# Grouped 1x1 convolution on one core: a loop of GpSimd memsets out, a narrow ring piece carried by four DMA engines in

## The chip, the core and the metric

The kernel runs on one core of a Trainium2 chip. The metric is device microseconds of that core for one execution. A time given for the kernel is the median of several executions; the profile and its trace come from one of them.

## The reference

An image of 512 x 512 pixels with 192 channels in bf16 goes through a 1x1 convolution in four groups of 48 channels. With k = 1 there is no padding, and the loop over window positions has one turn:

```python
xg = x.reshape(B, H, W, 4, 48)
out = einsum('bhwgc,gcd->bhwgd', xg, w[0, 0])      # w: 1 x 1 x 4 x 48 x 48
return out.reshape(B, H, W, 192)
```

So each of the 262,144 pixels is a row of 192 numbers (384 bytes) that is multiplied by a block-diagonal 192 x 192 matrix. The input is 100.66 MB and so is the output; every byte is read once and written once.

## The kernel before

**Layout.** Pixels are put on 128 rows (partitions) of SBUF. One *column* of a ring is one pixel on each of the 128 rows, 192 bf16 values wide. All pixels make 2048 columns. There are two rings of 256 columns, `x_sb` for input and `o_sb` for output. A *piece* is a run of columns that one transfer moves; row p of a piece of `size` columns is a contiguous run of `size` pixels in DRAM, so a piece of 64 columns moves 24,576 bytes for each row and 3,072 KB in all. `plan_pieces` cuts the 2048 columns into a head of 4, 4, 8, 16, 32 columns, then 30 pieces of 64 (`BIG`), then a tail of 32, 16, 8, 4, 4. Loads and stores use the same cut: 40 loads, 40 stores.

**Groups.** The compute engines work in groups of 4 columns, 512 groups in all, so a piece of 64 columns is 16 groups. For group g:

- TensorE transposes six 128 x 128 blocks of `x_sb` into `xT_ps` (line 203), three groups ahead of the products (`LOOK = 3`).
- VectorE copies them to `xT_sb` (line 260).
- TensorE multiplies with the block-diagonal weights `wt` into `o_ps`, six matmuls (line 226).
- ScalarE copies the result to `o_sb` (line 288, 128 x 768). In every fourth group VectorE takes half of it (line 266), and ScalarE the other half (line 285).

**Order and waits.** SyncE's queue issues all loads in order (line 175). A load waits until the groups that held its place in the ring, 64 groups before, have been transposed (`wq.wait(t_done, p.g1 - body)`). TensorE waits for a load's semaphore before the first transposes of its piece; a transfer adds 16 to its semaphore in increments of 1, one for each DMA engine that has finished. ScalarE's queue issues the stores (line 275), each two groups after the last group of its piece. Before writing group g to `o_sb`, ScalarE and VectorE wait until the store of the piece that held group g - 64 has landed (`wait_out_free`). TensorE's program has a loop of 7 turns over 64 groups, with unrolled groups ahead and behind; the other engines are unrolled. 

**GpSimd.** It builds `ident` and `esel`, two constant matrices, at the start. After that it runs the loop that the change removes: 63 turns of 64 memsets of one bf16 element of `scratch` (line 164), paced by four semaphores `pa_sem` that GpSimd alone sets and waits for. No other engine reads `scratch` or these semaphores.

**DMA.** The two queues (q1 for loads from SyncE, q10 for stores from ScalarE) run on the same 16 DMA engines. In a transfer of 128 rows each DMA engine carries 8 rows.

In the text a piece is called by its first column c: the piece c = 1600 holds groups 400 to 415.

Of the kernel before, what the change touches and what calls it, by code (L numbers as in the profile page):

```python
# [6 lines left out]
BF16 = mybir.dt.bfloat16  # L7
# [4 lines left out]
C = GROUPS * CG  # L12
# [12 lines left out]
BIG = 64  # L25
RCOLS = 256
HEAD = (4, 4, 8, 16, 32)
TAIL = (32, 16, 8, 4, 4)
# [2 lines left out]
LOOK = 3  # L31
ST_DELAY = 2
RING = 8


class Waiter:

    def __init__(self, eng):
        self.eng = eng
        self.seen = {}  # L40
# [7 lines left out]

class Piece:

    def __init__(self, col, size, key):
        self.col, self.size, self.key = col, size, key
        self.g0, self.g1 = col // 4, (col + size) // 4


def plan_pieces(cols, head, tail):
    sizes = list(head) if cols >= sum(head) + sum(tail) else []
    last = list(tail) if sizes else []
    mid = cols - sum(sizes) - sum(last)
    pieces, c = [], 0  # L60
    for s in sizes + [BIG] * (mid // BIG) + ([mid % BIG] if mid % BIG else []) + last:
        whole = s == BIG and c % BIG == 0
        pieces.append(Piece(c, s, ("big", c // BIG % (RCOLS // BIG)) if whole else ("own", len(pieces))))
        c += s
    return pieces


def bass_standalone__grouped__vision_kernel(nc, x, w, out):
    B, H, W_, Cx = x.shape
    assert Cx == C and tuple(w.shape) == (1, 1, GROUPS, CG, CG)  # L70
    npix = B * H * W_

    cols = npix // 128
    assert npix % 512 == 0, "the pixel count must be a multiple of 512"
    NG = cols // 4
    loads = plan_pieces(cols, HEAD, TAIL)
    stores = plan_pieces(cols, HEAD, TAIL)
    load_of = {p.g0: p for p in loads}
    store_at = {g: p for p in stores for g in range(p.g0, p.g1)}
    store_end = {p.g1 - 1: p for p in stores}  # L80
# [1 line left out]
    xf = x.rearrange("b h w c -> (b h w) c")  # L82
    of = out.rearrange("b h w c -> (b h w) c")
# [17 lines left out]
        if 0 <= h < NG and shared(h):  # L101
            dve_prog.append(("ev2", h))

    def rows_view(ap, p):
        return ap[128 * p.col:128 * (p.col + p.size), :].rearrange("(p i) c -> p (i c)", p=128)

    def ring_view(t, p):
        at = p.col % RCOLS
        assert at + p.size <= RCOLS
        return t[:, at * C:(at + p.size) * C]  # L110

    with ExitStack() as es:
        block = es.enter_context(nc.Block())
        x_sb = es.enter_context(nc.sbuf_tensor("x_sb", [128, RCOLS * C], BF16))
        o_sb = es.enter_context(nc.sbuf_tensor("o_sb", [128, RCOLS * C], BF16))
# [2 lines left out]
        esel = es.enter_context(nc.sbuf_tensor("esel", [CG, ECOLS], BF16))  # L118
        w_sb = es.enter_context(nc.sbuf_tensor("w_sb", [CG, GROUPS, CG], BF16))
        wt = es.enter_context(nc.sbuf_tensor("wt", [128, WCOLS], BF16))  # L120
        scratch = es.enter_context(nc.sbuf_tensor("scratch", [1, 64], BF16))
        xT_ps = es.enter_context(nc.psum_tensor("xT_ps", [128, NXP, 1024], BF16))
        o_ps = es.enter_context(nc.psum_tensor("o_ps", [128, NOB, 512], F32))

        def sem(name):
            return es.enter_context(nc.semaphore(name))

        ld_sem = {k: sem(f"ld_{k[0]}{k[1]}") for k in dict.fromkeys(p.key for p in loads)}
        st_sem = {k: sem(f"st_{k[0]}{k[1]}") for k in dict.fromkeys(p.key for p in stores)}
        st_val, seen = {}, {}  # L130
        for p in stores:
            seen[p.key] = seen.get(p.key, 0) + 16
            st_val[p] = seen[p.key]
        w_sem, id_sem, e_sem, wb_sem, wc_sem = (sem(s) for s in ("w_sem", "id_sem", "e_sem", "wb_sem", "wc_sem"))
        p0_sem, p1_sem = sem("p0_sem"), sem("p1_sem")
        pa_sem = [sem(f"pa_{i}") for i in range(4)]
        t_done, mm_done = sem("t_done"), sem("mm_done")
        e1_sem = [sem(f"e1_{i}") for i in range(RING)]
        fa_sem = [sem(f"fa_{i}") for i in range(RING)]
# [7 lines left out]
        @block.gpsimd  # L147
        def _(gp):
            gp.memset(esel[:], 1.0).then_inc(p0_sem, 1)  # L149
            gp.memset(ident[:], 1.0).then_inc(p1_sem, 1)  # L150
            gp.wait_ge(p0_sem, 1)
            gp.affine_select(out=esel[:], in_=esel[:], pattern=[[-1, ECOLS]],  # L152
                             compare_op=AluOpType.is_equal, fill=0.0, base=ESHIFT,
                             channel_multiplier=1).then_inc(e_sem, 1)
            gp.wait_ge(p1_sem, 1)
            gp.affine_select(out=ident[:], in_=ident[:], pattern=[[-1, 128]],  # L156
                             compare_op=AluOpType.is_equal, fill=0.0, base=0,
                             channel_multiplier=1).then_inc(id_sem, 1)
            gp.memset(scratch[:, 63:64], 0.0).then_inc(pa_sem[0], 1)  # L159
            with gp.Fori(0, 63, 1):  # L160
                for j in range(4):
                    gp.wait_ge(pa_sem[j], 1)
                    for i in range(16):
                        ins = gp.memset(scratch[:, j * 16 + i:j * 16 + i + 1], 0.0)  # L164
                        if i == 1:
                            ins.then_inc(pa_sem[j], -1)
                    ins.then_inc(pa_sem[(j + 1) % 4], 1)

        @block.sync
        def _(sp):  # L170
            wq = Waiter(sp)
            sp.dma_start(w_sb[:], wv).then_inc(w_sem, 16)  # L172
            for p in loads:
                wq.wait(t_done, p.g1 - body)
                sp.dma_start(ring_view(x_sb, p), rows_view(xf, p)).then_inc(ld_sem[p.key], 16)  # L175

        @block.tensor
        def _(pe):

            def build_weights():  # L180
                pe.wait_ge(e_sem, 1)
                pe.wait_ge(w_sem, 16)
                last = None
                for (tc, r, g, c0_) in WBLOCKS:
                    s0 = ESHIFT - r
                    col = WOFF[tc] + c0_
                    last = pe.matmul(o_ps[:, NOB - 1, col:col + CG], lhsT=esel[:, s0:s0 + 128],  # L187
                                     rhs=w_sb[:, g, :], start=True, stop=True, skip_group_check=True)
                last.then_inc(wb_sem, 1)

            def transposes(g):
                if g == 0:
                    pe.wait_ge(id_sem, 1)
                p = load_of.get(g)
                if p:
                    pe.wait_ge(ld_sem[p.key], 16)
                ins = []
                for ul in range(2):
                    u = g % body * 2 + ul
                    for tc in range(3):  # L200
                        col = u * UC + tc * 128
                        j = ul * 3 + tc
                        ins.append(pe.transpose(xT_ps[:, g % NXP, j * 128:(j + 1) * 128],  # L203
                                                x_sb[:, col:col + 128], ident[:]))
                if p:
                    ins[1].then_inc(ld_sem[p.key], -16)
                ins[-1].then_inc(t_done, 1)

            def matmuls(g):
                xs = xT_sb[g % NXP]  # L210
                waited = [e1_sem[g % RING]]
                if g == 0:
                    pe.wait_ge(wc_sem, 1)
                if g >= 2:
                    waited.append(fa_sem[(g - 2) % RING])
                    if shared(g - 2):
                        waited.append(d2_sem[(g - 2) // 4 % 2])
                for s in waited:
                    pe.wait_ge(s, 1)
                ins = []  # L220
                for ul in range(2):
                    v = 2 * g + ul
                    for tc in range(3):
                        j = ul * 3 + tc
                        c0_, c1_ = COLR[tc]
                        ins.append(pe.matmul(o_ps[:, v % NOB, c0_:c1_], lhsT=xs[:, j * 128:(j + 1) * 128],  # L226
                                             rhs=wt[:, WOFF[tc]:WOFF[tc] + (c1_ - c0_)],
                                             start=(tc == 0), stop=(tc == 2), skip_group_check=True))
                for i, s in enumerate(waited):
                    ins[1 + i].then_inc(s, -1)  # L230
                ins[-1].then_inc(mm_done, 1)

            def step(g):
                if g + LOOK < NG:
                    transposes(g + LOOK)
                matmuls(g)

            build_weights()
            for g in range(min(LOOK, NG)):
                transposes(g)  # L240
            for g in range(loop_g0 if reps else 0):
                step(g)
            if reps:
                with pe.Fori(0, reps, 1):
                    for g in range(loop_g0, loop_g0 + body):
                        step(g)
            for g in range(loop_g1 if reps else 0, NG):
                step(g)
# [21 lines left out]
        def _(act):  # L270
# [1 line left out]
            pending = []  # L272

            def store(p):
                act.dma_start(rows_view(of, p), ring_view(o_sb, p)).then_inc(st_sem[p.key], 16)  # L275

            for g in range(NG):
                wait_out_free(wq, g)
# [5 lines left out]
                if shared(g):  # L284
                    ins = act.copy(o_sb[:, u * UC:(u + 1) * UC], o_ps[:, v % NOB, 0:UC])  # L285
# [40 lines left out]
```

## Time and profile before

| | |
|---|---|
| median of 3 executions | 497.32 us (495.99 to 498.0) |
| the profiled execution's own time | 498.0 us |
| span of its profile | 496.3 us |
| granted TensorE clock | 0.95 |
| busy: TensorE matmul / weight load | 424.2 us (85%) / 408.8 us (82%) |
| busy: ScalarE / VectorE | 356.8 us (72%) / 336.9 us (68%) |
| busy: GpSimd | 148.4 us (30%), of it 147.1 us in 4032 memsets |
| DMA | 201.64 MB, 406 GB/s over the span |

The span is the profiler's, from the first instruction to the last event; the execution's own time is 1.7 us more. Busy shares are averages over the whole span. A step that lies beside other work costs nothing; what ends a wait, and what stands in the chain that ended last, tells what sets the time.

### The profile page before, as it was taken

To read this page: it belongs to the slowest core of one execution; us is meant where nothing else is said; L and a number is where in the kernel's file an instruction comes from. 1 tells how busy PE (TensorE), PEld (TensorE's weight loads), DVE (VectorE), ACT (ScalarE), POOL (GpSimd) and SP (SyncE) were. 2 spreads that over 40 slices of the span, in tenths; PEclk is the share of its full clock that TensorE was granted. 3 is DMA by queue.
4 is the path that set the end of the run, shared out by engine and by line. 5 is a ranking of instruction groups with operands and counts; after the bars stand their busy time and mean duration, and the time that the engine had idled before them with its cause. 6 is when DMAs were issued, how large, how long until landed. Compare 5 with 4: busy or idle time off the path is not lost.

```text
span 496.3 us, 18331 instructions
## 1 busy us (share of the span) xinstructions
PE 424.2 (85%) x6154; PEld 408.8 (82%) x6154; DVE 336.9 (68%) x640; ACT 356.8 (72%) x513; POOL 148.4 (30%) x4041
## 2 busy tenths in 40 slices
PE   5999998789887998797997797997979977999953
PEld 5989998788887998787997787987879977889852
DVE  3778877577675777576776576775767765778740
ACT  2888887577775778676787586776767865888752
POOL 8999999999999100000000000000000000000000
PEclk9999999899898999899899899898998998999986
DMA  8999999999999999999999999999999999995583
GB/s 295 432 423 425 429 427 436 426 432 434 425 431 429 432 434 428 432 431 432 430 426 429 432 430 424 432 430 430 430 426 434 430 420 436 427 381 243 223 365 144
DMA packets 11751, 201.64 MB, mean 406 GB/s; under 512 B 1488, under 2 KB 2512, under 8 KB 3536
## 3 DMA queue, kind: packets, MB, share of 16 engines
q1 hardware_dynamic: 5968, 100.68, 47.8%
q10 hardware_dynamic: 5760, 100.67, 47.7%
q8 instruction: 12, 0.20, 0.1%
q14 instruction: 11, 0.09, 0.0%
HBM read 100.68 MB, written 100.66 MB: 406 GB/s over the span
## 4 chain that ended last, share of the span: by engine, by line
DMA 83%; PE 12%; another core or an unknown queue 1%; ACT 1%; issue 1%; SPq 0%; ACTq 0%
DMA out_dram<-o_sb 81%; PE o_ps L226 7%; PE xT_ps L203 5%; DMA x_sb<-in_x_dram 1%; ACT o_sb L288 1%; SPq L175 0%; ACTq L275 0%; SPq L172 0%
## 5 line engine op out<-in xcount | busy, mean ns | idle before, releaser
L288 ACT CAST o_sb<-o_ps 128x768 bf16<-128x768 f32 x385 | 301.5, 798 | 123.7 <-PE o_ps L226 69.9
L260 DVE COPY xT_sb<-xT_ps 128x768 bf16<-128x768 bf16 x512 | 284.3, 555 | 112.8 <-PE xT_ps L203 105.8
L226 PE MATMUL o_ps<-wt,xT_sb 128*128 128x144 bf16 (+1 forms) x3072 | 308.3, 238 | 52.5 <-ACT o_sb L288 50.3
L203 PE MATMUL xT_ps<-ident,x_sb 128*128 128x128 bf16 x3072 | 266.0, 225 | 9.5 <-DMA x_sb<-in_x_dram 8.9
L226 PEld LDWEIGHTS o_ps<-wt,xT_sb 128*128 128x128 bf16 x3072 | 218.2, 100 | 65.9 <-issue 57.1
L203 PEld LDWEIGHTS xT_ps<-ident,x_sb 128*128 128x128 bf16 x3072 | 206.1, 101 | 11.2 <-DMA x_sb<-in_x_dram 9.2
L164 POOL MEMSET scratch<- 1x1 bf16 x4032 | 147.1, 91 | 14.4
L266 DVE CAST o_sb<-o_ps 128x384 bf16<-128x384 f32 x127 | 69.9, 551 | 32.9 <-DMA out_dram<-o_sb 30.6
L285 ACT CAST o_sb<-o_ps 128x384 bf16<-128x384 f32 x127 | 60.9, 480 | 8.8 <-PE o_ps L226 6.5
L256 DVE CAST wt<-o_ps 128x480 bf16<-128x480 f32 x1 | 0.7, 658 | 3.3 <-PE o_ps L187 3.3
L187 PE MATMUL o_ps<-w_sb,esel 48*128 48x48 bf16 x10 | 0.6, 210 | 2.8 <-DMA w_sb<-in_w_dram 2.8
L187 PEld LDWEIGHTS o_ps<-w_sb,esel 48*128 48x128 bf16 x10 | 0.5, 113 | 2.7 <-POOL esel L152 2.7
L288 ACT ACT_TABLE_LOAD x1 | 1.3, 1283 | 0.8 <-PEq L311 0.8
L152 POOL TENSOR_SCALAR_AFFINE_SELECT esel<-esel 48x272 bf16<-48x272 bf16 x1 | 0.4, 405 | 0.0
L149 POOL MEMSET esel<- 48x272 bf16 x1 | 0.3, 318 | 0.3 <-POOLq L311 0.3
L156 POOL TENSOR_SCALAR_AFFINE_SELECT ident<-ident 128x128 bf16<-128x128 bf16 x1 | 0.3, 285 | 0.0
L150 POOL MEMSET ident<- 128x128 bf16 x1 | 0.2, 198 | 0.0
L311 POOL MEMSET const-float32-0.0<- 128x1 f32 x1 | 0.1, 103 | 0.3 <-issue 0.3
L311 POOL MEMSET const-uint8-127<- 128x1 uint8 x1 | 0.1, 116 | 0.0
L311 POOL MEMSET const-bfloat16-1.0<- 128x1 bf16 x1 | 0.1, 113 | 0.0
L311 POOL MEMSET const-float32-1.0<- 128x1 f32 x1 | 0.1, 111 | 0.0
L159 POOL MEMSET scratch<- 1x1 bf16 x1 | 0.1, 91 | 0.0
## 6 DMA issues: line engine op xcount, KB each, us to landing
x_sb<-in_x_dram SPq DMA_DIRECT2D x30, 3072.0 KB, 28.9
out_dram<-o_sb ACTq DMA_DIRECT2D x30, 3072.0 KB, 45.5
x_sb<-in_x_dram SPq DMA_DIRECT2D x2, 1536.0 KB, 20.3
out_dram<-o_sb ACTq DMA_DIRECT2D x2, 1536.0 KB, 26.4
x_sb<-in_x_dram SPq DMA_DIRECT2D x2, 768.0 KB, 22.0
out_dram<-o_sb ACTq DMA_DIRECT2D x2, 768.0 KB, 19.8
x_sb<-in_x_dram SPq DMA_DIRECT2D x4, 192.0 KB, 27.2
x_sb<-in_x_dram SPq DMA_DIRECT2D x2, 384.0 KB, 24.6
```

Of the source, the lines that this page charges most:

```text
L149: gp.memset(esel[:], 1.0).then_inc(p0_sem, 1)
L152: gp.affine_select(out=esel[:], in_=esel[:], pattern=[[-1, ECOLS]], compare_op=AluOpType.is_equal, fill=0.0, base=ESHIFT, channel_multipli ...
L164: ins = gp.memset(scratch[:, j * 16 + i:j * 16 + i + 1], 0.0)
L187: last = pe.matmul(o_ps[:, NOB - 1, col:col + CG], lhsT=esel[:, s0:s0 + 128], rhs=w_sb[:, g, :], start=True, stop=True, skip_group_check=True)
L203: ins.append(pe.transpose(xT_ps[:, g % NXP, j * 128:(j + 1) * 128], x_sb[:, col:col + 128], ident[:]))
L226: ins.append(pe.matmul(o_ps[:, v % NOB, c0_:c1_], lhsT=xs[:, j * 128:(j + 1) * 128], rhs=wt[:, WOFF[tc]:WOFF[tc] + (c1_ - c0_)], start=(tc ...
L256: dve.tensor_copy(wt[:], o_ps[:, NOB - 1, 0:WCOLS]).then_inc(wc_sem, 1)
L260: dve.tensor_copy(xT_sb[g % NXP][:], xT_ps[:, g % NXP, 0:2 * UC]).then_inc(e1_sem[g % RING], 1)
L266: dve.tensor_copy(o_sb[:, u * UC:(u + 1) * UC], o_ps[:, v % NOB, 0:UC]).then_inc(d2_sem[g // 4 % 2], 1)
L285: ins = act.copy(o_sb[:, u * UC:(u + 1) * UC], o_ps[:, v % NOB, 0:UC])
L288: ins = act.copy(dst, o_ps[:, v % NOB:v % NOB + 2, 0:UC])
L311: nc = _bacc.Bacc("TRN2", target_bir_lowering=False, num_devices=1)
```

## The change

The memset loop, `scratch` and `pa_sem` go. In their place nothing is put on GpSimd.

The cut of the pixels changes. One piece of 64 columns is *narrow*: only rows 0 to 15 and 32 to 47 hold pixels (2048 of them, as many as 16 full columns), moved by two loads and two stores of 16 rows each, whose DRAM side has an outer dimension of 4. The other pixels fill 2032 full columns. With the narrow piece's 64 the ring runs over 2096 columns, so there are 524 groups instead of 512, and the compute engines treat the narrow piece's 16 groups like any others, on all 128 rows; of its results only the 32 rows are stored. A piece may no longer cross the ring's end, so the order is: head 4, 4, 8, 16, 32; 29 pieces of 64 (up to c = 1856); the narrow piece (c = 1920); then 48, 16, 16, 16, 8, 4, 4. That is 43 loads and 43 stores. A narrow transfer pair adds 32 to its semaphore, and TensorE waits for 32.

```diff
+FULL = ((0, 128),)
+NARROW = ((0, 16), (32, 16))
+N_NARROW = 1
...
+def plan_pieces(npix):
+    few = BIG * sum(rows for _, rows in NARROW)
+    n_few = N_NARROW if npix >= N_NARROW * few + 128 * (sum(HEAD) + sum(TAIL) + 8 * BIG) else 0
+    cols = (npix - n_few * few) // 128
...
+    sizes = [(s, FULL) for s in head + [BIG] * (mid // BIG)]
+    sizes += [(BIG, NARROW)] * n_few
+    sizes += [(s, FULL) for s in ([mid % BIG] if mid % BIG else []) + tail]
...
+    def transfers(ap, t, p):
         at = p.col % RCOLS
         assert at + p.size <= RCOLS
-        return t[:, at * C:(at + p.size) * C]
+        for (r0, rows, pix) in p.blocks:
+            px = ap[pix:pix + rows * p.size, :]
+            if p.narrow:
+                view = px.rearrange("(c a i) n -> a c (i n)", a=4, c=rows // 4)
+            else:
+                view = px.rearrange("(p i) n -> p (i n)", p=rows)
+            yield view, t[r0:r0 + rows, at * C:(at + p.size) * C]
...
-            gp.memset(scratch[:, 63:64], 0.0).then_inc(pa_sem[0], 1)
-            with gp.Fori(0, 63, 1):
-                for j in range(4):
-                    gp.wait_ge(pa_sem[j], 1)
-                    for i in range(16):
-                        ins = gp.memset(scratch[:, j * 16 + i:j * 16 + i + 1], 0.0)
-                        if i == 1:
-                            ins.then_inc(pa_sem[j], -1)
-                    ins.then_inc(pa_sem[(j + 1) % 4], 1)
...
-                sp.dma_start(ring_view(x_sb, p), rows_view(xf, p)).then_inc(ld_sem[p.key], 16)
+                for dram, ring in transfers(xf, x_sb, p):
+                    sp.dma_start(ring, dram).then_inc(ld_sem[p.key], 16)
...
-                act.dma_start(rows_view(of, p), ring_view(o_sb, p)).then_inc(st_sem[p.key], 16)
+                for dram, ring in transfers(of, o_sb, p):
+                    act.dma_start(dram, ring).then_inc(st_sem[p.key], 16)
```

More of the change, by code (lines that the diff above doesn't have):

```diff
@@ L49, with __init__ @@
 class Piece:
-    def __init__(self, col, size, key):
+    def __init__(self, col, size, key, blocks, pix):
         self.col, self.size, self.key = col, size, key
         self.g0, self.g1 = col // 4, (col + size) // 4
[L56 to L64, printed above, removed]
+        self.blocks = []
+        for (r0, rows) in blocks:
+            self.blocks.append((r0, rows, pix))
+            pix += rows * size
+        self.pix_end = pix
+        self.narrow = len(blocks) > 1
+def plan_pieces(npix):
+    few = BIG * sum(rows for _, rows in NARROW)
+    n_few = N_NARROW if npix >= N_NARROW * few + 128 * (sum(HEAD) + sum(TAIL) + 8 * BIG) else 0
+    cols = (npix - n_few * few) // 128
+    assert cols % 4 == 0
+    head, tail = (list(HEAD), list(TAIL)) if cols >= sum(HEAD) + sum(TAIL) else ([], [])
+    mid = cols - sum(head) - sum(tail)
+    sizes = [(s, FULL) for s in head + [BIG] * (mid // BIG)]
+    sizes += [(BIG, NARROW)] * n_few
+    sizes += [(s, FULL) for s in ([mid % BIG] if mid % BIG else []) + tail]
+    pieces, c, pix = [], 0, 0
+    while sizes:
+        s, blocks = sizes.pop(0)
+        room = RCOLS - c % RCOLS
+        if s > room:
+            sizes.insert(0, (s - room, blocks))
+            s = room
+        whole = s == BIG and c % BIG == 0 and blocks is FULL
+        key = ("big", c // BIG % (RCOLS // BIG)) if whole else ("own", len(pieces))
+        pieces.append(Piece(c, s, key, blocks, pix))
+        c, pix = c + s, pieces[-1].pix_end
+    assert pix == npix
     return pieces
@@ L71, in bass_standalone__grouped__vision_kernel @@
     npix = B * H * W_
-    cols = npix // 128
     assert npix % 512 == 0, "the pixel count must be a multiple of 512"
-    NG = cols // 4
-    loads = plan_pieces(cols, HEAD, TAIL)
-    stores = plan_pieces(cols, HEAD, TAIL)
+    loads = stores = plan_pieces(npix)
+    NG = loads[-1].g1
     load_of = {p.g0: p for p in loads}
@@ L102, in bass_standalone__grouped__vision_kernel @@
             dve_prog.append(("ev2", h))
-    def rows_view(ap, p):
-        return ap[128 * p.col:128 * (p.col + p.size), :].rearrange("(p i) c -> p (i c)", p=128)
-    def ring_view(t, p):
+    def transfers(ap, t, p):
         at = p.col % RCOLS
         assert at + p.size <= RCOLS
-        return t[:, at * C:(at + p.size) * C]
+        for (r0, rows, pix) in p.blocks:
[5 more added lines that the diff above has]
+            yield view, t[r0:r0 + rows, at * C:(at + p.size) * C]
     with ExitStack() as es:
@@ L120, in bass_standalone__grouped__vision_kernel @@
         wt = es.enter_context(nc.sbuf_tensor("wt", [128, WCOLS], BF16))
-        scratch = es.enter_context(nc.sbuf_tensor("scratch", [1, 64], BF16))
         xT_ps = es.enter_context(nc.psum_tensor("xT_ps", [128, NXP, 1024], BF16))
@@ L131, in bass_standalone__grouped__vision_kernel @@
         for p in stores:
-            seen[p.key] = seen.get(p.key, 0) + 16
+            seen[p.key] = seen.get(p.key, 0) + 16 * len(p.blocks)
             st_val[p] = seen[p.key]
@@ L135, in bass_standalone__grouped__vision_kernel @@
         p0_sem, p1_sem = sem("p0_sem"), sem("p1_sem")
-        pa_sem = [sem(f"pa_{i}") for i in range(4)]
         t_done, mm_done = sem("t_done"), sem("mm_done")
@@ L195, in transposes @@
                 if p:
-                    pe.wait_ge(ld_sem[p.key], 16)
+                    pe.wait_ge(ld_sem[p.key], 16 * len(p.blocks))
                 ins = []
@@ L205, in transposes @@
                 if p:
-                    ins[1].then_inc(ld_sem[p.key], -16)
+                    ins[1].then_inc(ld_sem[p.key], -16 * len(p.blocks))
                 ins[-1].then_inc(t_done, 1)
```

## The prediction

> **What bounds the kernel now.** I read the page's slices first: is the DMA full all the way?
>
> ```profile
> DMA  8999999999999999999999999999999999995583
> GB/s 295 432 423 425 429 427 436 426 432 434 425 431 429 432 434 428 432 431 432 430 426 429 432 430 424 432 430 430 430 426 434 430 420 436 427 381 243 223 365 144
> ```
>
> Up to slice 35 (434 us) the 16 DMA engines are full at about 430 GB/s. Then they are half idle, for 60 us. Bandwidth as a whole doesn't explain that end. The chain of work that ended last does (start, duration, what):
>
> ```profile
> 77.94 47.15 DMA out_dram<-o_sb
> 125.12 46.77 DMA out_dram<-o_sb
> ...
> 217.53 45.54 DMA out_dram<-o_sb
> 263.11 45.58 DMA out_dram<-o_sb
> 308.72 45.47 DMA out_dram<-o_sb
> 354.22 45.55 DMA out_dram<-o_sb
> ...
> 478.36 6.17 another core or an unknown queue
> ```
>
> From store to store, each link 45 us or more, and each spans three ring pieces, so 15.2 us for one piece (64 columns loaded and 64 stored). A 24,576-byte packet takes 912 ns at the median in the packet records; 8 for the load and 8 for the store are 14.6 us. Something runs 4% slower than the typical DMA engine. The trace's completion increments (16 for each transfer, one for each DMA engine) name it: of the last load, fourteen came by 445.4 us, the fifteenth at 447.4, the sixteenth at 484.5. Of store c = 1600, fourteen by 419.7 and the last at 443.6. In all loads and stores after 70 us **one DMA engine comes last alone**, by 7 to 10 us in loads and up to 23 in stores. It also ends the run: its last stores land at 488.3, 492.1, 493.9, 494.8, 495.3 and 495.8, while the other fifteen are done by 492.4. Those steps are its packets back to back. It works from the first load to the end without a gap, so its bytes times its pace are the time. The waits up to 440 us and after agree:
>
> ```profile
> ACT o_sb L288 <- DMA out_dram<-o_sb: 51.5, 24, 3.3
> ...
> PE xT_ps L203 <- DMA x_sb<-in_x_dram: 6.2, 1, 6.2
> ```
>
> ScalarE waits for stores once for each piece; at the end TensorE waits 6.2 us for the last load (the chain's "unknown queue" at 478.36), which stood behind the late engine's stores.
>
> Second reading: the pace differs. The late engine's increments for loads come each 15.72 us from 70.0 to 164.3 us (six steps), and each 15.19 us from 179.6 to 437.8 (seventeen). The chain says the same: 47.15, then 45.5. What ends in between?
>
> ```profile
> L164 POOL MEMSET scratch<- x4032: 91/91/94, 2.1 to 163.4; 1x1 bf16 x192
> ```
>
> ```profile
> 60.00:160.00 100.00, 85.43 (x1244) 82.38 (x1242) 68.13 (x130) 71.62 (x105) 91.06 (x2499) 0.95 1.00 430
> 160.00:400.00 240.00, 210.13 (x3054) 203.50 (x3051) 167.29 (x318) 175.78 (x254) 3.24 (x90) 0.95 1.00 430
> ```
>
> The last memset starts at 163.4 us. In these windows (PE, PEld, DVE, ACT, POOL busy with counts, clock, DMA share, GB/s) nothing but GpSimd's 2499 instructions changes; the typical packet stays at 912 ns, and the late engine's store packets go from about 1040 to 985 ns.
>
> Third reading, the tail's compute, from the timeline:
>
> ```profile
> 445.22 2.35 ACT L288 CAST o_sb<-o_ps 128x768 bf16<-128x768 f32 x3 [0.38 <-PE o_ps L226]
> 448.33 2.35 ACT L288 CAST o_sb<-o_ps 128x768 bf16<-128x768 f32 x3 [0.33 <-PE o_ps L226]
> ```
>
> Four groups in 3.11 us, 0.78 a group: unhindered, a piece takes 12.5 us, under the 15.2 of the late engine. From 443.66 us (store c = 1600 has landed) to 478.36 compute runs at this pace without a stop.
>
> [...]
>
> **The change part by part.**
>
> *Twelve DMA engines carry less.* 2032 instead of 2048 full columns, 16 fewer each way. On the late engine: 16/64 x 15.19 = **3.8 us less**, if it isn't one of the four.
>
> *Four engines carry more.* 2096 columns, 48 more: 48/64 x 14.6 = 10.9 us. They had 512 packets' worth each way, 64 x 8 x 0.912 = 467 us; with this 478, and from the first load at 4.9 us that is 483 without a gap. The late engine's end will be 488 (below), and after 440 us they were idle for about half of the time. Cost 0; it decides if they get more than 5 us of idle time that the late one has not.
>
> *The memset loop goes.* Measured on the chain: (47.15 - 45.54) + (46.77 - 45.54) = 2.8 us. Before 77.9 us the loop ran too; 3.4% of the chain's first store link (39.4 us) is 1.35 more. **4.2 us less**. Bounds: 0 if something else changed at 160 us, 5.5 if all of 2.1 to 163.4 us ran 3.4% slow. A loss could only come if the memsets sped something, and nothing slows after 163 us. GpSimd has no other work.
>
> *Twelve more groups*, 9.4 us of compute at 0.78. Ahead of the tail it lies beside DMA. In the tail it doesn't: see the sum.
>
> *Queues and waits.* SyncE issues 43 loads for 40, but waited 408.6 us for TensorE; 0. ScalarE issues 3 more stores at 0.34 us: up to 1.0 us in the tail. TensorE's wait for 32 has the products of group 477 and on behind it; the four engines have the narrow load before about 435 us and group 480 comes at about 451: 0, and up to 7 us if it were late. No later group reuses the narrow piece's output place.
>
> *The sum.* Late engine: 495.8 - 3.8 - 4.2 = 487.8 us. Compute: store c = 1536, which frees group 448, landed at 430.1, now at 425.9. Its 16 groups take 12.5 us, to 438.4. Store c = 1600 landed at 443.6, now at 437.5 to 439.4 (4.2 earlier, and up to 1.9 for the shorter load ahead of it). So group 464 starts at 438.4 to 439.4; 60 groups to the end at 0.78 are 46.8: 485.2 to 486.2. Add 1.0 for the issues and 2.1 from ScalarE's end to the landing (490.1 to 492.2 before): 488.3 to 489.3. The last load now lands in time, since no big store stands beside it: the 6.2 us wait goes, and **compute is late next, by about a microsecond**. The span ends 0.5 after the last landing: 489.3, which is 7.0 under 496.3. The profiled execution took 498.0, 0.7 above the median; off its 498.0 the sum gives 491.0, off the median **490.3**, which I give.
>
> **Rivals.**
>
> 1. *The loop's end and the new pace are a coincidence.* For: no shared buffer or semaphore is seen. Against: the step falls within one piece of the last memset, in every packet after it. The engine's end is 492.0; compute starts 4.2 later and ends the span at 493.5: saving 2.8, 494.5.
> 2. *The transfers don't stay on four engines* but spread over 16. Then the late engine's bytes don't change: 495.8 - 4.2 = 491.6, span 492.1, saving 4.2: 493.1.
> 3. *The late engine is one of the four* (slower). It gets 48/64 x 15.19 = 11.4 us more, less 4.2: 7.2 slower, 504.5. The trace doesn't tell which engine is late; four of sixteen would be 1 in 4[...]. It decides by that alone.
> 4. *The tail costs more*, with a load of the small pieces behind a store again (6.2 us before): about 496.5.
>
> **How the numbers follow.** Both parts as said: 0.61, own range 487 to 493 (the memset term 0 is rival 1, at 5.5 it is 1.3 less; the tail 2 either way). Rivals 1 to 4: 0.12, 0.06, 0.13, 0.08. The range 486.5 to 496.5 takes in all but rival 3 and the far ends. A measurement can tell 0.5%, 2.5 us, from no change. Faster: the first case and rivals 1 and 2, 0.79; same 0.07; slower 0.14.
>
> **What would show it.** Right: chain links of 45.5 us from the first on; load increments 15.2 us apart before 160 us; the last engine's final landing near 488; two transfers of 384 KB in which 12 increments come at once; no 6 us wait for the last load, and compute gapless from about 439 us. Wrong: links still at 47 early on (rival 1), or the late engine's last landing beyond 500 us (rival 3).

## The result, and the profile after

The changed kernel takes 491.18 us (median of 4, 490.61 to 491.86) beside 496.65 us for the kernel before (a fourth execution of it, 495.75 us, has joined the three behind the 497.32 given above): ratio 0.9888, 95% interval 0.9857 to 0.9919. A second time, in the experiments, it took 490.95 us beside 495.88: 0.9909, interval 0.9883 to 0.9935. It is faster by 0.9 to 1.1%, 4.5 to 5.5 us. The profiled execution took 491.86 us, with a span of 490.1.

The slices of its page:

```profile
DMA  7999999999999999999999999999999999999557
GB/s 268 432 426 430 427 430 431 433 431 433 428 433 426 437 425 435 427 436 427 435 429 434 429 431 431 432 427 435 429 433 428 431 429 426 424 424 390 218 217 306
```

The DMA's digit is 9 through slice 37 (453 us), where before it was through slice 36 (447 us) of a longer span; then come two half-empty slices, and a rise in the last one, where before the last one was the emptiest. The end has another shape. The chain of work that ended last (start, duration, what):

```profile
51.60 39.08 DMA out_dram<-o_sb
90.71 45.19 DMA out_dram<-o_sb
135.93 45.42 DMA out_dram<-o_sb
181.38 45.55 DMA out_dram<-o_sb
...
363.57 45.54 DMA out_dram<-o_sb
409.13 0.81 ACT o_sb L302
...
456.30 1.07 issue
...
463.68 1.34 issue
```

No link is above 45.6 us any more, not even before 160 us: the 47.15 and 46.77 of before are gone. From 409.13 us the chain has no transfer in it at all. It runs through TensorE and ScalarE to the end, with two stops ("issue": TensorE waited for nothing that the profile shows); the second begins while ScalarE's queue issues the two narrow stores (462.52 to 464.41 us). The waits from 440 us on:

```profile
ACT o_sb L302 <- PE o_ps L239: 4.5, 11, 1.2
PEld o_ps L239 <- issue: 4.2, 5, 1.5
ACT o_sb L299 <- issue: 3.0, 5, 1.8
```

Neither a load nor a store ends a wait there; the 6.2 us for the last load are gone. The late DMA engine is still there: its last load lands at 474.3 us, 7.7 after the fifteenth engine's (37 before), and its last store at 489.6, the others' at 488.3. But ScalarE no longer waits for it after 409 us.

### The profile page after: what moved, and what is told of

Read it like the earlier page. It is cut to its first block, busy times and chain, and to the rows that moved or that the text cites. A ratio compares the mean times of both kernels' runs of the same rounds, so it can differ in the third digit from the quotient of the medians.

```text
span 490.1 us, 14506 instructions
## 1 busy us (share of the span) xinstructions
PE 430.6 (88%) x6298; PEld 415.3 (85%) x6298; DVE 344.4 (70%) x655; ACT 365.4 (75%) x525; POOL 1.3 (0%) x8
## 4 chain that ended last, share of the span: by engine, by line
DMA 77%; PE 18%; ACT 3%; issue 1%; SPq 1%; ACTq 0%
DMA out_dram<-o_sb 73%; PE o_ps L239 10%; PE xT_ps L216 7%; DMA x_sb<-in_x_dram 4%; ACT o_sb L302 3%; SPq L188 0%; ACTq L289 0%; ACT o_sb L299 0%; SPq L184 0%; ACTq L49 0%
## 5 line engine op out<-in xcount | busy, mean ns | idle before, releaser
L302 ACT CAST o_sb<-o_ps 128x768 bf16<-128x768 f32 x394 | 308.5, 798 | 106.2 <-PE o_ps L239 60.3
L273 DVE COPY xT_sb<-xT_ps 128x768 bf16<-128x768 bf16 x524 | 291.0, 555 | 108.6 <-PE xT_ps L216 101.2
L239 PE MATMUL o_ps<-wt,xT_sb 128*128 128x144 bf16 (+1 forms) x3144 | 313.6, 237 | 45.9 <-ACT o_sb L302 43.3
L216 PE MATMUL xT_ps<-ident,x_sb 128*128 128x128 bf16 x3144 | 270.8, 224 | 5.6 <-DMA x_sb<-in_x_dram 4.6
L239 PEld LDWEIGHTS o_ps<-wt,xT_sb 128*128 128x128 bf16 x3144 | 221.5, 99 | 59.5 <-issue 50.5
L216 PEld LDWEIGHTS xT_ps<-ident,x_sb 128*128 128x128 bf16 x3144 | 209.6, 101 | 7.1 <-DMA x_sb<-in_x_dram 4.4
L279 DVE CAST o_sb<-o_ps 128x384 bf16<-128x384 f32 x130 | 71.6, 551 | 26.0 <-DMA out_dram<-o_sb 24.5
L299 ACT CAST o_sb<-o_ps 128x384 bf16<-128x384 f32 x130 | 62.4, 480 | 13.5 <-PE o_ps L239 7.6
## 6 DMA issues: line engine op xcount, KB each, us to landing
out_dram<-o_sb ACTq DMA_DIRECT2D x29, 3072.0 KB, 45.5
```

The lines of the kernel that those rows point to most:

```text
L273: dve.tensor_copy(xT_sb[g % NXP][:], xT_ps[:, g % NXP, 0:2 * UC]).then_inc(e1_sem[g % RING], 1)
L279: dve.tensor_copy(o_sb[:, u * UC:(u + 1) * UC], o_ps[:, v % NOB, 0:UC]).then_inc(d2_sem[g // 4 % 2], 1)
L302: ins = act.copy(dst, o_ps[:, v % NOB:v % NOB + 2, 0:UC])
```

## The experiments

Every ratio is to the kernel before on the same chip. Times differ by some 0.5% between executions of one kernel (495.33 to 498.11 us in 35 of before), and a trace shows one execution. So a difference of 1 us, between two medians or between the landings in two traces, isn't shown by itself; what comes last within one trace is.

**1. The loop alone out.**

```diff
-            gp.memset(scratch[:, 63:64], 0.0).then_inc(pa_sem[0], 1)
-            with gp.Fori(0, 63, 1):
...
```

> The kernel before without the memset loop, nothing else changed. Theory: the memsets slow the one late DMA engine, whose bytes times its pace set the end. Then the completion increments of loads come 15.15 us apart from the start, and the store of piece c = 1600 lands about 5.8 us earlier than before (443.6), as far ahead as the changed kernel was in mid-run; the engine's last landing goes from 495.8 to about 490, the time to about 491 us (ratio 0.988). Rival, coincidence: the pace is 15.7 us up to 160 us and the time 496.6 as before; the whole gain of the changed kernel came from the narrow piece.

492.14 us (6 executions), ratio 0.9915 (0.9894 to 0.9936), which is 4.2 us of 495.96. The chain of this kernel:

```profile
77.02 43.79 DMA out_dram<-o_sb
120.84 45.53 DMA out_dram<-o_sb
```

The link that was 47.15 us is 43.79, three pieces at the 14.6 us of the typical engine. That the late one has hardly fallen behind yet in this stretch is an estimate from the changed kernel, which has no loop either: there its store increments come 0.02 us after the fifteenth at 90.7 us and 0.94 at 120.7. From the next link on the pace is the later one. Store c = 1600 lands at 438.0 us, 5.6 earlier; the late engine's last landing is 490.1. Its last load still comes alone, at 478.9 us against 453.8 for the fifteenth engine, and TensorE waits 6.3 us for it. Coincidence is out: most of the gain is the loop's. The median is 1 us above the expected 491.

**2. The loop three times as long.**

```diff
-            with gp.Fori(0, 63, 1):
+            with gp.Fori(0, 189, 1):
```

> The kernel before with three times as many turns of the memset loop (189), so that it runs to about 484 us. Theory: the pace of the late engine stays at 15.7 us for each piece to the end; from 163 to 484 us that is 21 pieces by 0.55 us, 11 us more: 507 to 508 (ratio 1.022). Rival, coincidence at 160 us: 15.2 us after 170 us as before, 496.6.

508.55 us, ratio 1.0249 (1.0231 to 1.0268). The memset row and the chain:

```profile
L164 POOL MEMSET scratch<- x12096: 91/92/95, 2.1 to 487.2; 1x1 bf16 x199
```

```profile
171.00 47.13 DMA out_dram<-o_sb
218.17 47.11 DMA out_dram<-o_sb
...
359.76 46.90 DMA out_dram<-o_sb
```

While GpSimd runs memsets a link is 46.9 to 47.1 us, 15.7 for each piece; where it ran none, 45.5. The time is half a us above the expected 507 to 508. The pace follows the loop in both directions.

**3. Fewer, wider memsets.** What of a memset slows the engine?

```diff
-        scratch = es.enter_context(nc.sbuf_tensor("scratch", [1, 64], BF16))
+        scratch = es.enter_context(nc.sbuf_tensor("scratch", [128, 64 * 56], BF16))
...
-            with gp.Fori(0, 63, 1):
+            with gp.Fori(0, 24, 1):
...
-                        ins = gp.memset(scratch[:, j * 16 + i:j * 16 + i + 1], 0.0)
+                        ins = gp.memset(scratch[:, (j * 16 + i) * 56:(j * 16 + i + 1) * 56], 0.0)
```

> The kernel before with 24 turns instead of 63 of the loop (1536 memsets), each of 128 rows by 56 elements instead of one element, 14 KB instead of 2 bytes. What of the memsets slows the late engine? If it is the number of instructions for each us (25 before; here, at some 140 ns each, 7 to 10), the excess pace is a third of 0.55 us, so about 15.35 us for each piece while the loop runs, and the time about 493.5. If it is what they write to SBUF, thousands of times as much, the pace is 15.7 us or far more while the loop runs.

493.35 us, ratio 0.9941 (0.9923 to 0.9958). The memset row, and two links of the chain, inside the loop and after it:

```profile
L164 POOL MEMSET scratch<- x1536: 144/144/147, 2.1 to 136.5; 128x56 bf16 x192
```

```profile
90.78 46.09 DMA out_dram<-o_sb
...
197.65 45.53 DMA out_dram<-o_sb
```

46.09 us for three pieces are 15.36 each. The rate was 1536 in 134 us, 11.4 for each us, against 25; 7,168 times as many bytes in each memset. The excess over 45.53 is 0.56 us, a third of the 1.6 at 25 instructions for each us. So the excess doesn't grow with what the memsets write; it falls with their number. The number alone would give 11.4/25 of 1.6, 0.73 us, so it fits only roughly. The loop's semaphore waits and increments fell in the same proportion as its memsets, and no run tells these apart.

**4. The narrow piece alone** (the changed kernel with the loop put back).

> The changed kernel with the memset loop put back. Theory: the pace is 15.7 us for each piece up to about 163 us, then 15.15; the late engine has 16 columns less each way, 3.8 us; the end is at 492 to 493.5 (late engine or the compute of 12 more groups), the time 493 to 494.5 (ratio 0.993 to 0.996). Rival, the narrow piece does all: 491 (0.989). Rival, the narrow piece does nothing because the tail gives it back: 496.6.

495.58 us (22 executions), ratio 0.9989 (0.9981 to 0.9998): 0.5 us, where 1.5 to 3 were expected. The rival by which the tail gives the gain back was nearly right. From 413.83 us on (store c = 1472 has landed) its chain has no transfer in it, as that of the changed kernel from 409.13: the tail is compute and the last stores here too, only that it starts later. The late engine's last landing is 492.8 us, 1.2 after the fifteenth engine's, where it was 3.4 before.

**5. An outer dimension of 16 instead of 4.**

```diff
-                view = px.rearrange("(c a i) n -> a c (i n)", a=4, c=rows // 4)
+                view = px.rearrange("(c a i) n -> a c (i n)", a=16, c=rows // 16)
```

> The changed kernel with an outer dimension of 16 instead of 4 in the narrow piece's transfers, one row for each DMA engine. Theory: the four-engine confinement is what relieves the late engine; spread over 16 it carries as much as before the change, 3.8 us more than in the changed kernel. Its last landing moves from 489.6 to between 490 and 492 us (part of the 3.8 fell into its idle time there), time 492 to 493; no increments of the narrow transfers come at once from the queue, and their two store issues take about 0.34 us each instead of 1.9 together. Rival, the confinement never mattered or never took place: same landings and 491.2.

496.59 us (14 executions), ratio 1.0004 (0.9991 to 1.0017), more than expected. The late engine carries 16 columns more again. Its last load lands at 486.6 us, the fifteenth engine's at 456.3, TensorE waits 4.0 us for it, and the kernel ends at 494.8. The completion increments show the spreading: the two narrow loads have 32 recorded increments here, as two transfers of 128 rows have in the traces; with the outer 4 they have 10. In the changed kernel's trace two of these come first, at 403.9 and 404.9 us, and eight between 414.6 and 423.3. Each load adds 16 in all, so with 1 for each of four engines the early one stands for the other twelve; the trace doesn't give the amounts, and this is the author's reading of the counts. The DMA's busy share agrees: from 465.0 to 473.4 us the changed kernel has little more than its narrow stores and the late engine's last big store to carry, and the share is 0.28, 4.5 engines of 16. So the confinement takes place, and the piece is useful only with it. This run and experiment 1, on one chip, have the same bytes on every DMA engine; the twelve groups more and the other tail make the time 496.59 us instead of 492.14. So the narrow piece costs some 4.4 us that the confinement has to win back before anything is gained.

**6. An outer dimension of 8** (`a=8, c=rows // 8` in the same line). By the author's estimate each narrow transfer then runs on eight engines. Two cases were set apart: 491 us if the late engine isn't among the eight, 495 to 498 if it is one of them and wasn't one of the four.

> The changed kernel with an outer dimension of 8: [...] 4 row-loads of 24,576 bytes each way and engine instead of 8 on four. [...] its bytes are those of the changed kernel and the time is the same, 491 (fewer engines are loaded less, the tail by compute stays). [...] it carries 32 columns more each way than in the changed kernel, 7.6 us, of which up to 2.5 fall into its idle time near the end: 495 to 498.

498.46 us, ratio 1.0044 (1.0028 to 1.0060): about 7 us above the changed kernel, just above the 495 to 498 expected. The increments are 18, nine for each transfer: by the same reading eight engines, and one increment for the other eight. The last load's sixteenth increment comes at 488.0 us and its fifteenth at 463.8. In the narrow load itself the last increment comes alone, 3.8 us after the one before it, and with an outer 4 it doesn't (0.55 us). So the late engine is among the eight that an outer 8 uses, and the times and increments with an outer 4 say it isn't among those four.

**7. The narrow piece six pieces earlier.**

```diff
-    sizes += [(BIG, NARROW)] * n_few
+    sizes[len(sizes) - EARLIER:len(sizes) - EARLIER] = [(BIG, NARROW)] * n_few     # EARLIER = 6
```

(TensorE's loop ends ahead of it.)

> The changed kernel with the narrow piece moved ahead of the last six pieces of 64 columns (c = 1536 instead of 1920); its 16 groups and the two issues of its store then lie far from the tail. Theory: the changed kernel ends late by compute, not by the late DMA engine, which idles around 474 us; with the 12 extra groups under the DMA the late engine sets the end again: last landing 486 to 487 us, time about 488 (ratio to before 0.982). Rival: the end is the row of stores of the last 112 columns (48, 16, 16, 16, 8, 4, 4), which starts when the 48-column piece is issued, and nothing ahead of it matters: 491 as with the change (0.989).

491.69 us, ratio 0.9903 (0.9875 to 0.9931), not told apart from the changed kernel; the expected 488 didn't come. The late engine catches up fully at the narrow piece (the next load lands at 347.7 us, the fifteenth engine's at 347.5), but the DMA then has gaps: slices 32 and 33 of the page fall to 363 and 393 GB/s. From 406.86 us on its chain runs through compute as well.

**8. Less work in twelve of the narrow piece's groups** (2 of 6 transposes, 5 of 6 matmuls, copies of 8 elements).

> The changed kernel with the work of 12 of the narrow piece's 16 groups cut down: 2 of 6 transposes, 5 of 6 matmuls, copies of 8 elements instead of 384 or 768. What these groups should compute is left out. Transfers, waits and their order stay. A group then takes about 0.48 us on TensorE instead of 0.78. Theory: the changed kernel ends late by the compute of its last 92 groups; 12 x 0.3 = 3.6 us less puts the 48-column store's issue 3 to 3.6 us earlier, the end is then set by the late DMA engine at about 487: time 487.5 to 488.5. Rival, the late DMA engine or the row of stores sets the end whatever compute does: 491 as in the changed kernel.

490.38 us, ratio 0.9883 (0.9866 to 0.9899); expected 487.5 to 488.5. From the issue of store c = 1856 to that of the narrow one it takes 11.8 us, where the changed kernel takes 13.7 on the same chip (experiment 11): 1.9 us were taken away, not 3.6. TensorE stood still for 1.9 us ("issue" at 459.54 in its chain) among the lighter groups, and this execution came to them 2.9 us later. Its interval overlaps that of the changed kernel on this chip (0.9883 to 0.9935). It decides nothing.

**9. The narrow piece without any groups** (its own place at c = 2048, the same four transfers, 508 groups; its load now goes last, and its store follows that of c = 1792).

```diff
-    sizes += [(BIG, NARROW)] * n_few
...
+    narrow = Piece(2048, BIG, ("own", 99), NARROW, pix)
...
-    NG = loads[-1].g1
+    NG = loads[-2].g1
```

> The changed kernel, but the narrow piece has no groups: it has its own place at the end of the ring's count (c = 2048), is loaded and stored by the same four transfers, and no engine computes on it, so there are 508 groups instead of 524. What the narrow piece's 2048 pixels should give is left out. The bytes of each DMA engine are those of the changed kernel. Theory: the changed kernel ends by the compute of its last 92 groups and the row of stores behind it; with 16 groups by 0.78 us less, 12.5 us, the late DMA engine sets the end again, and all that it gained shows: last landing 486 to 487.5, time 487.5 to 489. Rival, compute does not matter and the end is the DMA's own: 491 as in the changed kernel.

490.08 us, ratio 0.9878 (0.9862 to 0.9895). Its waits from 400 us on:

```profile
PEld xT_ps L219 <- DMA x_sb<-in_x_dram: 9.8, 3, 5.5
PE xT_ps L219 <- DMA x_sb<-in_x_dram: 9.1, 3, 5.3
```

With compute out of the way the waits for the late engine's loads are back (its last load lands at 479.5 us, the fifteenth engine's at 468.0). It ends at 487.7 us, with all sixteen engines within 0.2 us of each other, because the last stores wait for compute, and that for the late loads. The changed kernel ended at 489.6 and, in experiment 11, at 489.0. By these traces the narrow piece's compute costs it 1.3 to 1.9 us; the medians don't show it, since the interval here overlaps both of the changed kernel. The time fell by less than expected.

**10. A narrow piece of 32 columns** (`SMALL = 32`; 8 columns taken from twelve engines).

> The changed kernel with a narrow piece of 32 columns instead of 64: 8 columns taken from twelve engines instead of 16, 6 more groups than before the change instead of 12. Theory: what the late DMA engine gains (1.9 us instead of 3.8) and what compute loses at the end (6 groups by 0.78, 4.7 us, instead of 9.4) meet between the loop-free kernel before (490.6 span) and the changed one (490.1): late engine 488.1, compute 2 to 4 us earlier than in the changed kernel; time 489 to 490.5, a little under the changed kernel. Rival, more narrow columns are always better: 492, above the changed kernel.

492.56 us, ratio 0.9930 (0.9913 to 0.9947). The median is above the changed kernel's on this chip, as the rival had it, but the intervals overlap, and its profiled execution, the fastest of six, ends at 488.5 us, earlier than the changed kernel's. Which width is better stays open.

**11. The changed kernel again**, as a reference.

> The changed kernel once more, as the reference for the two others on the same chip: 0.989 of the kernel before, 491 us, compute without a stop from the landing of store c = 1472 (about 409 us) to the end.

490.95 us; 0.9909. Its last wait for a store ends at 422.54 us, and compute runs on from there, 13 us later than expected; the end is the same, 489.0.

**12. The 48-column piece cut in three.**

```diff
-    sizes += [(s, FULL) for s in ([mid % BIG] if mid % BIG else []) + tail]
+    sizes += [(s, FULL) for s in [16] * (mid % BIG // 16) + tail]
```

> The changed kernel with its 48-column piece cut into three of 16. Theory: in the changed kernel all DMA engines stand nearly idle until the 48-column store is issued at 473.4 us, and the stores of the last 112 columns then go back to back to the end, behind compute. With pieces of 16 the first of these stores goes out about 6 us earlier, the stores keep up with compute, and the end is ScalarE's last copy plus one small store: 488.0 to 489 instead of 489.6, time 489.5 to 490.5. Rival, two more issues and small pieces cost what they bring: 491 to 492.

489.99 us (489.68 to 490.73), ratio 0.9880 (0.9863 to 0.9896). In the changed kernel ScalarE's queue issues the 48-column store late:

```profile
473.36 0.34 ACTq L289 DMA_DIRECT2D out_dram<-o_sb  x1
...
484.70 0.34 ACTq L289 DMA_DIRECT2D out_dram<-o_sb  x1
485.10 1.24 ACTq L289 DMA_DIRECT2D out_dram<-o_sb  x2
```

Cut in three, the first of them goes out 6.4 us earlier:

```profile
466.97 0.33 ACTq L289 DMA_DIRECT2D out_dram<-o_sb  x1
470.09 0.34 ACTq L289 DMA_DIRECT2D out_dram<-o_sb  x1
473.22 0.34 ACTq L289 DMA_DIRECT2D out_dram<-o_sb  x1
...
484.93 1.14 ACTq L289 DMA_DIRECT2D out_dram<-o_sb  x2
```

All sixteen engines then end within 0.2 us of each other, at 488.0 against 489.6 and 489.0, although ScalarE issues its last store at the same time (485.7 us against 485.9). It has the lowest median of the kernels that compute everything, but its interval overlaps the changed kernel's.

## Why the prediction was right, point by point

**One DMA engine sets the time: right for the kernel before.** Its pace carries the time up with a longer loop (experiment 2), and its bytes do with an outer 8 or 16 (5 and 6). Two details were read loosely, without effect: in loads the engine is 0.8 us late at 70 us and 7 to 10 only from 148 us on, and the 512 packets of 467 us are 256 each way.

**The memset loop, 4.2 us: right, the match in the last digit by luck.** Alone it gave 0.85%, 4.2 us (0.64 to 1.06%). The traces put the gain in mid-run higher: store c = 448 landed at 171.9 us before and at 166.2 after, 5.7 us, mainly because the first link lost 3.4 us (experiment 1) where 1.6 were counted. That the median shows less fits the execution of before that was profiled, which was 2 us slower than its median (see the total). The first rival, coincidence, is refuted by experiments 1 to 3.

**The narrow transfers stay on four engines, and the late one isn't among them: right,** shown by 5 and 6: 32, 18 and 10 increments with an outer 16, 8 and 4, and the late engine's last load at 486.6, 488.0 and 474.3 us. These were rivals 2 and 3. Rival 3 was near: at an outer dimension of 8, with half as many bytes for the late engine, it comes true and the kernel is slower than before. That an outer dimension of 4 keeps the transfers on four engines was the author's estimate; no trace of before showed it, nor which engine is late. So the odds of rival 3 were nearer 1 in 4 than the 0.13 given, and that the four missed the late engine was luck to that extent.

**Late engine's end 487.8: not contradicted.** Without the narrow piece's groups the end is 487.7 (experiment 9), but there all engines end together behind a wait for the late loads, so the match isn't a test of this term alone.

**Compute is late next, by about a microsecond: right as a mechanism, a little small.** The end of the row was to be 488.3 to 489.3; it was 489.6 and 489.0. Three terms were off and nearly cancelled:

- The start. Group 464's copy was to start at 438.4 to 439.4 us; in the changed kernel it did at about 435.7, since ScalarE's last wait ended at 409.13 and the stores c = 1536 and 1600 landed at 422.9 and 435.4 us, just before it came to their places (425.9, and 437.5 to 439.4, in the sum).
- The 60 groups. 46.8 + 1.0 was the sum; from 435.7 to ScalarE's end at 485.88 it took 50.2. The two narrow stores hold ScalarE's queue for 1.9 us where two issues at 0.34 were counted, and TensorE stood still once, so that ScalarE waited 1.2 us. Such a stop was in the profile before as well, in the stretch that the prediction read as one without a stop:

```profile
464.30 1.08 issue
```

After the change:

```profile
457.91 1.55 ACT L302 CAST o_sb<-o_ps 128x768 bf16<-128x768 f32 x2 [1.18 <-PE o_ps L239]
...
462.52 1.89 ACTq L289 DMA_DIRECT2D out_dram<-o_sb  x2
464.45 0.48 ACT L299 CAST o_sb<-o_ps 128x384 bf16<-128x384 f32 x1 [1.82 <-issue]
```

- The landing. From ScalarE's end it took 3.7 us and not 2.1. The 48-column store is issued at 473.36 us, when the late engine has just landed its last big one (473.4) and most others have been idle (the fifteenth landed its at 464.8, the narrow stores end at 473.9, and the DMA's share from 465.0 to 473.4 us is 0.28); after it the stores of 112 columns stand in a row. The sum followed compute to its last copy and overlooked that this store, not the last one, begins the end. Cutting it in three starts the row earlier, and the end is 2.3 us after ScalarE's last copy (12).

**The total: forecast 7.0 us less, measured 4.5 to 5.5.** The sum of parts gave the narrow piece 2.8 us of net gain. Alone it gave 0.5 (experiment 4); on top of the missing loop, 0.9888 and 0.9909 against 0.9915, 0.3 to 1.3, and these intervals overlap. That is the mis-sized term: a net gain of the narrow piece on top of the missing loop isn't shown. Of the 3.8 us of fewer bytes, 2.4 show where the narrow piece has no compute (an end of 490.1 us in experiment 1, of 487.7 in 9), and compute and the store row take back 1.3 to 1.9 of these, each read from single traces. A part of the rest is the base: the spans before and after differ by 6.2 us, but the profiled execution of before, 498.0, was one of its longest (495.33 to 498.11 in 35 executions, median 495.96). The prediction took 0.7 us off for that; against the larger sample it is 2.

**Open.** Why instructions of GpSimd slow one DMA engine isn't shown. The other engines together run about as many instructions for each us as the loop did (some 27 against 25, counted in the windows from 60 to 160 us of before), and without the loop the late engine is 0.6 us for each piece slower than the typical 14.6, with it 1.1. That would fit a cost for each instruction of any engine; it wasn't tried. Every execution on record was also a profiled one, with its span and its granted clock, so the runs don't tell whether the recording of instructions has a part in it, or whether the engine is as late without it.

## What to carry to other kernels

When bandwidth is full and yet one transfer always lands late, look at the sixteen completion increments, not at their mean: here one engine of sixteen set the time, its last load 37.1 us after the fifteenth's, and its bytes and its pace were what to change. Then price the end of the run separately: here compute, which had lain beside the transfers, became the bound from 409.13 us on when they were shortened, and it was the first large store behind it, not the last small one, that began the final row. Measure each part of a change alone: here the loop brings nearly all of the gain, and the narrow piece wins back little more than it costs. Compare a saving with the median of many executions before quoting it from two profiles.

## What the runs showed of the hardware that was not expected

- The time of one DMA engine rose with the number of GpSimd instructions: 15.2 us for each piece with none (before, after the loop), 15.36 at 11 for each us (experiment 3), 15.7 at 25 (experiment 2), although those at 11 wrote 14 KB each and those at 25 wrote 2 bytes.
- The narrow stores held ScalarE's queue longer on fewer than 16 engines: their two issues took 1.89 us on four engines (the changed kernel) and 1.98 on eight (experiment 6), 0.81 on sixteen (experiment 5); the issue of a store of 128 rows took 0.34.
- TensorE stood still once for 1.07 us, waiting for nothing that the profile shows, at the same place of its unrolled groups with and without the change: 20.6 us after the start of group 464's copy (at 464.30 us before, 458.60 in experiment 1, 456.30 after).
